# Dealing the last 1024 columns of wq's eighth rows to DMA engines by two indirect loads

## The chip, the cores and the metric

The kernel runs on one core of one Trainium2 chip. The metric is the device time of one execution, in microseconds (us). A core has five engines that run side by side: TensorE (PE), VectorE (DVE), ScalarE (ACT), GpSimd (POOL) and SyncE (SP). SP, ACT and GpSimd also issue DMAs, and these are carried out by 16 DMA engines that the three share.

## The reference, cut to what matters

One decode step for four sequences: an attention block over the last 2048 positions of a cache, then a gated feed-forward block. Layernorm stands in front of both. All inputs are bfloat16.

```python
B, D, Hq, Hkv, Dh, Sk, W, F = 4, 1024, 32, 4, 128, 8192, 2048, 3584
x  = A_x                                   # (4, 1, 1024)
q  = layernorm(x) @ wq                     # wq: (1024, 4096)
s  = q . k_cache[:, :, Sk - W:] * Dh**-0.5 # each of 4 kv heads serves 8 q heads
o  = softmax(s) . v_cache[:, :, Sk - W:]
h  = x + o @ wo                            # wo: (4096, 1024)
n  = layernorm(h)
out = h + (silu(n @ w1) * (n @ w3)) @ w2   # w1, w3: (1024, 3584); w2: (3584, 1024)
```

In all 55.6 MB are read from HBM and 8 KB are written.

## The kernel before

**One stream of weights.** Every weight and cache block goes through one ring in SBUF (`ring`, 128 partitions of 160 KiB). The list `plan` has the loads in order: wq's rows 0 to 3 of each partition, two side loads, wq's rows 4 to 7 (`load_tail`), the four K blocks, the four V blocks, wo, w1, w3 and w2 in four pieces. `load_next` issues the next ones on SP's queue. Seven entries are issued at the start; each later one is issued at a point of the program at which the ring's old contents in its place have been read. In program order SP waits with the load until that reading is done. So w1's issue waits for the attention output of batches 0 and 1 (`OT_ps`, L379), w3's for row 11 of the wo product (L408) and w2's for the wo product and for w1.

**wq.** `wq` is seen as 128 partitions of eight rows: partition p holds rows 8p to 8p + 7, so row 8p + 7 is its eighth row, `kc` = 7. The q product (L263) takes one `kc` after the other. Each time all 128 partitions of the ring meet `xnT[:, kc, :]`, the transposed normalized input, and add into `q_ps` in PSUM: four column groups of 1024 by two halves of 512.

**The side loads.** The last 512 columns of all the eighth rows (`CE` = 512) are left out of `load_tail`. They come by two loads (`load_side`, L120) into tiles of 20 and of 12 partitions, four rows in each partition, 80 + 48 = 128 pieces of 1 KB. To multiply them, the matching elements of `xn` are picked (`xs`, L206), transposed (L211) and copied (`xsT`, L218). Eight matmuls of 20 or 12 rows (L273) add them into `q_ps` after the `kc` = 3 step.

**Behind q.** q is scaled (L281, L282), transposed (L285) and laid out in `qz` (L286). Then K blocks are transposed on TensorE (L319), copied out by VectorE (L322) and multiplied with q (L304). Softmax, the product with V (L379), the wo product (L408), the second layernorm and the feed-forward block (L456, L489) follow. The result goes out by one DMA (L512).

**At the start.** GpSimd makes the identity matrix (`make_identity`, masks.py) and sets `o4` (L237) and `ones` (L242). ACT's queue loads x in two halves (`x_sb`, L158). VectorE clears `x_q`, `q_ps` and `qz`, takes the statistics of x (L180, L182) and normalizes it (L187); TensorE transposes it (L194) and VectorE copies it to `xnT` (L196).

A scheduler decides the order of instructions on each engine from their dependences. Each engine, and each queue, then works through its own list in order.

Of the kernel before, what the change touches and what calls it, by code (L numbers as in the profile page):

```python
# [10 lines left out]
P = 128  # L11
ACT = mybir.ActivationFunctionType
ALU = mybir.AluOpType
AX = mybir.AxisListType
BF16 = mybir.dt.bfloat16
FP32 = mybir.dt.float32


@with_exitstack
def kernel(  # L20
# [13 lines left out]
    nc = tc.nc  # L34

    B, _, D = A_x.shape
# [5 lines left out]
    KC = D // P  # L42
# [15 lines left out]
    ktpool = ctx.enter_context(tc.tile_pool(name="ktpool", bufs=4))  # L58
    wide = ctx.enter_context(tc.tile_pool(name="wide", bufs=2))
    const = ctx.enter_context(tc.tile_pool(name="const", bufs=1))  # L60
    act = ctx.enter_context(tc.tile_pool(name="act", bufs=1))
# [3 lines left out]
    JG = 4  # L65
    QD = P // JG
    RS = QD // B
    CQ = Hq * Dh // JG
# [40 lines left out]
    N_Q, N_F = Hq * Dh, F  # L109


    CE = 512
    SETS = [(0, 5, 4), (80, 3, 4)]

    def load_side(r0, ne, ns):

        t = ktpool.tile([P, JG * QD * 16], BF16, tag="kT")
        rows = A_wq[r0 * KC : (r0 + ne * 4 * ns) * KC, N_Q - CE : N_Q]
        rows = rows.rearrange("(t i k) n -> k i t n", i=ne, k=KC)[KC - 1]
        nc.sync.dma_start(out=t[: ne * 4, : ns * CE], in_=rows)  # L120
        return [t[: ne * 4, k * CE : (k + 1) * CE] for k in range(ns)]

    def load_tail(at, src, n, r0, m):

        t = ring[:, at : at + m * n]
        nc.sync.dma_start(out=t[:, : m * n - CE], in_=src[:, r0 * n : (r0 + m) * n - CE])
        return [t[:, k * n : (k + 1) * n] for k in range(m)]
    KIB = 512
    plan = [
        ("wq", load_rows, (0, wq_v, N_Q, 0, 4)),  # L130
        ("side", load_side, SETS[0]),
        ("side", load_side, SETS[1]),
        ("wq", load_tail, (32 * KIB, wq_v, N_Q, 4, 4)),
        ("k", load_kv, (64 * KIB, A_k_cache, 0)),
        ("k", load_kv, (96 * KIB, A_k_cache, 2)),
# [10 lines left out]
    loaded = {}  # L146
    cursor = [0]

    def load_next(n=1):
        for _ in range(n):  # L150
            if cursor[0] < len(plan):
                kind, f, args = plan[cursor[0]]
                loaded.setdefault(kind, []).extend(f(*args))
                cursor[0] += 1

    x_sb = act.tile([B, D], BF16)
    for c in range(2):
        nc.scalar.dma_start(out=x_sb[:, c * 512 : (c + 1) * 512], in_=x_flat[:, c * 512 : (c + 1) * 512])  # L158
    load_next(7)

    ident = const.tile([P, P], BF16)
    make_identity(nc, ident[:])
    eps_t = const.tile([P, 1], FP32)
    nc.vector.memset(eps_t[:], eps)

# [2 lines left out]
    for c in range(2):  # L168
        nc.sync.dma_start(
            out=x_q[c * 2 * QD : (c + 1) * 2 * QD : RS, :],  # L170
            in_=x_flat.rearrange("b (j c) -> j b c", j=JG)[2 * c : 2 * c + 2],
# [3 lines left out]
    psA = psA_cm.__enter__()  # L175


    stats = act.tile([B, 2, nc.vector.BN_STATS_DIM], FP32)
    for c in range(2):
        nc.vector.bn_stats(out=stats[:, c, :], in_=x_sb[:, c * 512 : (c + 1) * 512])  # L180
    mv = act.tile([B, nc.vector.BN_AGGR_DIM], FP32)
    nc.vector.bn_aggr(out=mv[:], in_=stats[:])  # L182
    rstd = act.tile([B, 1], FP32)
    nc.scalar.activation(out=rstd[:], in_=mv[:, 1:2], func=ACT.Sqrt, bias=eps_t[:B], scale=1.0)
    nc.vector.reciprocal(out=rstd[:], in_=rstd[:])
    xn = act.tile([B, D], BF16)
    nc.vector.tensor_scalar(  # L187
        out=xn[:], in0=x_sb[:], scalar1=mv[:, 0:1], scalar2=rstd[:, 0:1],
        op0=ALU.subtract, op1=ALU.mult,
# [5 lines left out]
    xnT = act.tile([P, KC, B], BF16)  # L195
    nc.vector.tensor_copy(out=xnT[:], in_=tp_ps[:])  # L196


    NS = sum(ns for _, _, ns in SETS)
    ts_ps = psA.tile([P, NS, B], BF16, tag="kt1")  # L200
    xs = wide.tile([B, NS, 20], BF16, tag="w4k")
    sl = []
    for r0, ne, ns in SETS:
        v = xn[:, r0 * KC : (r0 + ne * 4 * ns) * KC]
        v = v.rearrange("b (s l i k) -> b k l i s", s=4, l=ns, i=ne)
        nc.vector.tensor_copy(  # L206
            out=xs[:, len(sl) : len(sl) + ns, : ne * 4].rearrange("b l (i s) -> b l i s", s=4),
            in_=v[:, KC - 1, :, :, :],
        )
        for l in range(ns):  # L210
            nc.tensor.transpose(  # L211
                out=ts_ps[: ne * 4, len(sl), :], in_=xs[:, len(sl), : ne * 4], identity=ident[:B, :B]
            )
            sl.append(ne * 4)
    xsT = act.tile([20, NS, B], BF16)
    k0 = 0
    for _, ne, ns in SETS:
        nc.vector.tensor_copy(out=xsT[: ne * 4, k0 : k0 + ns, :], in_=ts_ps[: ne * 4, k0 : k0 + ns, :])  # L218
        k0 += ns


    q_ps = psA.tile([P, CQ], FP32, tag="scores")
    nc.vector.memset(q_ps[:], 0.0)

    qz = act.tile([P, B, Hkv * QD + REP], BF16)
    nc.vector.memset(qz[:], 0.0)
    ident_f = const.tile([P, P], FP32)
    nc.vector.tensor_copy(out=ident_f[:], in_=ident[:])
# [3 lines left out]
        out=perm[:].rearrange("p (h dq) -> p h dq", dq=JG),  # L232
        in_=ident[:].rearrange("p (dq h) -> p h dq", dq=JG),
    )

    o4 = act.tile([P, IO, B, RS], BF16)
    nc.gpsimd.memset(o4[:], 0.0)  # L237

    mask = const.tile([P, Hkv], FP32)
    nc.vector.reduce_sum(out=mask[:], in_=ident[:].rearrange("p (pp g) -> p g pp", g=Hkv), axis=AX.X)  # L240
# [5 lines left out]
    for j in range(2, JG):  # L246
        nc.vector.tensor_tensor(
            out=same[:, 0, :], in0=same[:, 0, :], in1=ident[:, j * QD : (j + 1) * QD], op=ALU.add
# [6 lines left out]
    for kc in range(KC):  # L255
        wq_t = loaded["wq"][kc]
        for hf in range(CQ // 512):
            for g in range(JG):
                c0 = g * CQ + hf * 512
                n = min(512, N_Q - CE - c0) if kc == KC - 1 else 512  # L260
                if n <= 0:
                    continue
                nc.tensor.matmul(  # L263
                    q_ps[QD * g : QD * g + B, hf * 512 : hf * 512 + n],
                    lhsT=xnT[:, kc, :],
                    rhs=wq_t[:, c0 : c0 + n],
                    start=(kc == 0),
                    stop=(kc == KC - 1 or (kc == KC - 2 and c0 + 512 == N_Q)),
                )
        if kc == RQ - 1:  # L270
            load_next()
            for k, np_ in enumerate(sl):
                nc.tensor.matmul(  # L273
                    q_ps[QD * (JG - 1) : QD * (JG - 1) + B, CQ - CE : CQ],
                    lhsT=xsT[:np_, k, :],
                    rhs=loaded["side"][k],
                    start=False,
                    stop=False,
                )
    q_sb = act.tile([P, CQ], BF16)  # L280
    nc.vector.tensor_single_scalar(out=q_sb[:, :512], in_=q_ps[:, :512], scalar=qscale, op=ALU.mult)  # L281
    nc.scalar.mul(out=q_sb[:, 512:], in_=q_ps[:, 512:], mul=qscale)  # L282
# [1 line left out]
    for r in range(REP):  # L284
        nc.tensor.transpose(out=qt_ps[:, r, :], in_=q_sb[:, r * Dh : (r + 1) * Dh], identity=ident[:])  # L285
    nc.vector.tensor_copy(  # L286
        out=qz[:, :, : Hkv * QD].rearrange("p b (g z) -> p b g z", g=Hkv)[:, :, :, :REP],
        in_=qt_ps[:].rearrange("p r (g x) -> p x g r", g=Hkv)[:, :B, :, :],
# [24 lines left out]
    for u, (b, n) in enumerate(units):  # L313
        k_v = loaded["k"][b]
        kT = ktpool.tile([P, NJ, P], BF16, tag="kT")
        for t in range(NJ // TB):
            kt_ps = psA.tile([P, TB, P], BF16, tag=f"kt{nt % 4}")
            for jj in range(TB):
                nc.tensor.transpose(  # L319
                    out=kt_ps[:, jj, :], in_=k_v[:, n * NJ + t * TB + jj, :], identity=ident[:]  # L320
# [18 lines left out]
        out=Pm[:], in_=scores_ps[:], func=ACT.Exp, bias=nmax[:], scale=1.0, accum_out=rsum[:]  # L339
# [6 lines left out]
    for c in range(NSB):  # L346
# [4 lines left out]
        for g in range(Hkv):  # L351
            if g % 2 == 0:
                nc.vector.tensor_scalar(  # L353
                    out=z[:, :, g, :], in0=pt_ps[:], scalar1=mask[:, g : g + 1], scalar2=None, op0=ALU.mult
# [10 lines left out]
        out=Dm[:], in0=ident[:].rearrange("p (g b r) -> p b g r", g=Hkv, b=B),  # L365
        scalar1=rinv[:, 0:1], scalar2=None, op0=ALU.mult,
# [10 lines left out]
    for b in range(B):  # L377
        for j in range(JK):
            nc.tensor.matmul(  # L379
                OT_ps[:, b, :],  # L380
                lhsT=loaded["v"][b][:, j, :],
                rhs=PTz[j // NJ][:, (j % NJ) * B + b, :, :],
                start=(j == 0),
                stop=(j == JK - 1),
# [21 lines left out]
    for i in range(IO):  # L406
        for j in range(JG):
            nc.tensor.matmul(  # L408
                y_ps[QD * j : QD * (j + 1), :],
                lhsT=o4[:, i, :, :].rearrange("p b s -> p (b s)"),  # L410
                rhs=loaded["wo"][i][:, j * CG : (j + 1) * CG],
                start=(i == 0),
                stop=(i == IO - 1),
# [27 lines left out]
        out=hn[:], in0=h1[:], scalar1=tot[:, 0:1], scalar2=rstd2[:, 0:1],  # L441
        op0=ALU.subtract, op1=ALU.mult,
# [4 lines left out]
        out=hnT[:].rearrange("p k x -> p (k x)"), in_=hn[:].rearrange("q (c k) -> q k c", k=KC)  # L447
# [3 lines left out]
    def gate_up(kind, out_ps):  # L451
# [27 lines left out]
        out=hgT[:].rearrange("p i x -> p (i x)"),  # L479
        in_=hg[:].rearrange("q s c -> q (s c)").rearrange("q (c i) -> q i c", i=IF),  # L480
# [18 lines left out]
    for i in range(R1, IF):  # L499
        for c, t in enumerate((ya_ps, yb_ps)):  # L500
            down(i, HC, c * HC, t, start=(i == R1), stop=(i == IF - 1), skip_group_check=True)
        if i == R2 - 1:
            for c, t in enumerate((ya_ps, yb_ps)):
                nc.tensor.matmul(
                    t[:, :HC], lhsT=ident_f[:], rhs=h2[:, c * HC : (c + 1) * HC],
                    start=False, stop=False, skip_group_check=True,
# [36 lines left out]
```

## Time and profile before

| | us |
|---|---|
| Median of 3 runs | 138.02 (137.87 to 138.12) |
| The profiled execution's own time | 137.67 |
| Its span, first to last instruction | 135.9 |
| First ring load of wq lands, first q matmul | 12.87 |
| Second ring load of wq lands, matmuls go on | 23.61 |
| w1 is issued; its first matmul | 72.82; 98.77 |
| w3's first matmul | 115.67 |
| w2's first matmul | 126.04 |
| Last group of w2 matmuls begins | 132.66 |

Busy shares of the span: TensorE 49%, VectorE 39%, ScalarE 11%, GpSimd 1%; SP's DMA queue holds the 16 DMA engines for 95.6% of it. The page is of one execution, times in us from the span's start. In the row "DMA" each digit is the busy share, in tenths, of one fortieth of the span. The table of DMA queues gives the number of packets, the megabytes, and the time of the packets as a share of 16 engines' span: q1 is SP's queue, q10 is ACT's, q8 and q14 carry instructions. The chain that ended last is followed back from the last instruction, and shown in order of time as start, duration and what. In the timeline each line has start, duration, engine, line of the kernel, operation, output<-inputs, shape and count, and in brackets the idle time before it and what ended that.

### The profile page before, as it was taken

The numbers are of one execution on the slowest core, as the hardware profiler recorded it, in microseconds if no ns is written. First come the engines' busy times: TensorE is split into PE (matmuls) and PEld (weight loads), VectorE is DVE, ScalarE is ACT, GpSimd is POOL, SyncE is SP. The second block draws the span as 40 slices with busy tenths as digits, with TensorE's granted clock in tenths as the row PEclk, the third lists the DMA queues.
The fourth block names the chain that finished last, engine by engine and source line by source line (L and its number), as shares of the span: only waits on it lengthen the run. The fifth ranks groups of instructions, "written<-read, shape, count | busy, mean of one in ns | idle before, by whom it ended". The sixth has DMA issues, their size and how long they took to land.

```text
span 135.9 us, 2420 instructions
## 1 busy us (share of the span) xinstructions
PE 66.7 (49%) x1096; PEld 42.1 (31%) x1096; DVE 53.2 (39%) x95; ACT 15.1 (11%) x20; POOL 1.7 (1%) x8
## 2 busy tenths in 40 slices
PE   0004930979898989105259155930094000940961
PEld 0002210266656565001149053720041000410750
DVE  6056000069696969709940003044000893052010
ACT  3000000010000000092943000000005000000000
POOL 5000000000000000000000000000000000000000
PEclk9999985699999999955555955599559955599599
DMA  5999999999999999999989999989989899899970
GB/s 156 464 463 415 404 430 405 434 424 439 420 439 415 434 439 415 424 550 439 482 347 444 487 405 410 439 376 490 456 371 477 354 490 408 379 451 399 414 317 2
DMA packets 2649, 55.74 MB, mean 410 GB/s; under 512 B 296, under 2 KB 464, under 8 KB 720
## 3 DMA queue, kind: packets, MB, share of 16 engines
q1 hardware_dynamic: 2604, 55.58, 95.6%
q8 instruction: 8, 0.13, 0.3%
q10 hardware_dynamic: 36, 0.02, 0.1%
q14 instruction: 1, 0.01, 0.0%
HBM read 55.59 MB, written 0.01 MB: 409 GB/s over the span
## 4 chain that ended last, share of the span: by engine, by line
DMA 57%; PE 22%; DVE 10%; ACT 6%; SPq 2%; issue 1%; ACTq 0%
DMA ring<-in_B_w_dram 42%; DMA ring<-in_A_wq_dram 15%; PE kt_ps L319 10%; PE scores_ps L304 5%; DVE kT L322 4%; DVE z L353 3%; ACT z L357 3%; PE q_ps L263 2%; PE g_ps L456 2%; DVE rmax L333 2%; ACT Pm L338 2%; PE OT_ps L379 1%; DVE pT L347 1%; SPq L120 1%; ACT L338 1%
## 5 line engine op out<-in xcount | busy, mean ns | idle before, releaser
L322 DVE COPY kT<-kt_ps 128x1024 bf16<-128x1024 bf16 x32 | 20.2, 685 | 5.2 <-PE kt_ps L319 5.0
L319 PE MATMUL kt_ps<-ident,ring 128*128 128x128 bf16 x256 | 16.5, 219 | 0.0
L319 PEld LDWEIGHTS <-ring 128*128 128x128 bf16 x256 | 14.4, 98 | 5.0 <-issue 4.9
L379 PE MATMUL OT_ps<-z,ring 128*128 128x32 bf16 x256 | 7.5, 186 | 9.6 <-ACT z L357 5.0
L456 PEld LDWEIGHTS <-hnT 128*32 128x32 bf16 x128 | 4.6, 121 | 24.0 <-issue 20.6
L304 PE MATMUL scores_ps<-kT,qz 128*32 128x512 bf16 x64 | 9.9, 609 | 1.7 <-DVE kT L322 1.5
L456 PE MATMUL u_ps<-ring,hnT 128*32 128x448 bf16 x64 | 4.6, 459 | 12.4 <-DMA ring<-in_B_w_dram 12.4
L379 PEld LDWEIGHTS <-ring 128*128 128x128 bf16 x256 | 7.3, 103 | 10.3 <-issue 10.2
L263 PE MATMUL q_ps<-ring,xnT 128*4 128x512 bf16 x63 | 6.8, 603 | 7.3 <-DMA ring<-in_A_wq_dram 7.3
L456 PE MATMUL g_ps<-ring,hnT 128*32 128x448 bf16 x64 | 4.5, 455 | 7.4 <-DMA ring<-in_B_w_dram 7.4
L489 PEld LDWEIGHTS <-hgT 128*32 128x32 bf16 x156 | 4.1, 113 | 8.2 <-issue 7.6
L281 DVE TENSOR_SCALAR q_sb<-q_ps 128x512 bf16<-128x512 f32 x1 | 0.7, 692 | 14.3 <-PE q_ps L263 14.3
L489 PE MATMUL y_ps<-ring,hgT 128*32 128x256 bf16 x68 | 3.4, 382 | 5.8 <-DMA ring<-in_B_w_dram 5.8
L408 PE MATMUL y_ps<-ring,o 128*32 128x256 bf16 x128 | 5.7, 364 | 0.8 <-DVE o L395 0.8
L353 DVE TENSOR_SCALAR z<-pt_ps,mask 128x512 bf16<-128x512 f32 x8 | 5.5, 740 | 1.1 <-ACT z L357 0.8
L470 DVE RECIPROCAL eg<-eg 128x896 f32<-128x896 f32 x1 | 5.8, 5752 | 0.0
L357 ACT ACTIVATE z<-pt_ps,mask 128x512 bf16<-128x512 f32 x8 | 5.4, 687 | 3.4 <-DVE z L353 3.4
L349 PE MATMUL pt_ps<-pT,perm 128*128 128x512 bf16 x4 | 2.4, 608 | 6.8 <-DVE pT L347 6.8
L194 PE MATMUL tp_ps<-ident,xn 4*128 4x4 bf16 x8 | 0.7, 199 | 10.0 <-DVE xn L187 10.0
L263 PEld LDWEIGHTS <-xnT 128*4 128x4 bf16 x63 | 2.1, 116 | 11.2 <-issue 11.1
L469 DVE TENSOR_SCALAR eg<-eg 128x896 f32<-128x896 f32 x1 | 0.6, 627 | 12.1 <-ACT eg L468 12.1
L408 PEld LDWEIGHTS <-o 128*32 128x32 bf16 x128 | 4.3, 129 | 3.0 <-DVE o L395 1.9
(84 smaller groups left out, 47.1 us busy)
## 6 DMA issues: line engine op xcount, KB each, us to landing
ring<-in_B_w_dram SPq DMA_DIRECT2D x2, 7168.0 KB, 25.9
ring<-in_A_k_cache_dram SPq DMA_DIRECT2D x4, 2048.0 KB, 27.6
ring<-in_A_v_cache_dram SPq DMA_DIRECT2D x4, 2048.0 KB, 29.1
ring<-in_B_w_dram SPq DMA_DIRECT2D x1, 4352.0 KB
ring<-in_A_wq_dram SPq DMA_DIRECT2D x1, 4096.0 KB, 12.1
ring<-in_A_wq_dram SPq DMA_DIRECT2D x1, 3968.0 KB
ring<-in_B_w_dram SPq DMA_DIRECT2D x1, 1792.0 KB
ring<-in_B_w_dram SPq DMA_DIRECT2D x1, 768.0 KB
```

Source lines behind the costliest of these rows:

```text
L263: nc.tensor.matmul(q_ps[QD * g : QD * g + B, hf * 512 : hf * 512 + n], lhsT=xnT[:, kc, :], rhs=wq_t[:, c0 : c0 + n], start=(kc == 0), stop ...
L304: nc.tensor.matmul(scores_ps[QD * g : QD * (g + 1), n * 512 : (n + 1) * 512], lhsT=qz_v[:, z0 : z0 + QD], rhs=kT_v[:, g, :, :], start=(b = ...
L319: nc.tensor.transpose(out=kt_ps[:, jj, :], in_=k_v[:, n * NJ + t * TB + jj, :], identity=ident[:])
L322: nc.vector.tensor_copy(out=kT[:, t * TB : (t + 1) * TB, :], in_=kt_ps[:])
L338: nc.scalar.activation(out=Pm[:], in_=scores_ps[:], func=ACT.Exp, bias=nmax[:], scale=1.0, accum_out=rsum[:])
L353: nc.vector.tensor_scalar(out=z[:, :, g, :], in0=pt_ps[:], scalar1=mask[:, g : g + 1], scalar2=None, op0=ALU.mult)
L357: nc.scalar.mul(out=z[:, :, g, :], in_=pt_ps[:], mul=mask[:, g : g + 1])
L379: nc.tensor.matmul(OT_ps[:, b, :], lhsT=loaded["v"][b][:, j, :], rhs=PTz[j // NJ][:, (j % NJ) * B + b, :, :], start=(j == 0), stop=(j == J ...
L408: nc.tensor.matmul(y_ps[QD * j : QD * (j + 1), :], lhsT=o4[:, i, :, :].rearrange("p b s -> p (b s)"), rhs=loaded["wo"][i][:, j * CG : (j + ...
L456: nc.tensor.matmul(out_ps[QD * j : QD * (j + 1), hf, :HF], lhsT=hnT[:, k, :], rhs=loaded[kind][k][:, c0 : c0 + HF], start=(k == 0), stop=( ...
L470: nc.vector.reciprocal(out=eg[:], in_=eg[:])
L489: nc.tensor.matmul(out_ps[QD * j : QD * (j + 1), :n], lhsT=hgT[:, i, :], rhs=loaded["w2"][i][:, j * CG + c0 : j * CG + c0 + n], **kw,)
```

## The change

The eighth rows lose their last 1024 columns (`CX`) in the ring load. These come as 128 pieces of 2 KB by two indirect loads on GpSimd's queue, into a tile `xg` of 128 partitions and two layers. `DEAL` lists, for each of the two loads, which runs of slots (partitions of `xg`) take a piece: 82 slots in the first load and 46 in the second. The wq rows are numbered off into these slots in order.

The matrix `sel` has a one where row m goes to slot s, and is copied together from columns of the identity on GpSimd. A matmul of `sel` with the row numbers minus 256 (`pv`) gives each slot its row number, from which VectorE computes the block index (`idf`, `idx`). A slot without a row gets an index past `bounds_check`, and is left out by the load. A matmul of `sel` with `xnT[:, 7, :]` gives each slot its factor of x (`xgT`), zero for empty slots, and `xg` is cleared at the start. Four matmuls over 128 slots add the product into `q_ps`, behind the `kc` = 7 step.

With it go: the side loads, their picking, transposes, copies and matmuls. One more of the last row's matmuls goes (both halves of the last column group are now left out). The clearing of `o4` moves from GpSimd to VectorE, and the normalization's `stats` tile shares its buffer with `idf`.

In the changed program's lists, VectorE has the clearing of `xg` first, and `idf` and `idx` ahead of the statistics of x. GpSimd has `sel`'s clearing, the identity, the row numbers, `ones`, twelve copies into `sel`, the cast of the row numbers and then the two loads. SP's list is the same without the two side loads. TensorE begins with the two matmuls for the indices.

```diff
-    CE = 512
-    SETS = [(0, 5, 4), (80, 3, 4)]
-    def load_side(r0, ne, ns):
-        t = ktpool.tile([P, JG * QD * 16], BF16, tag="kT")
-        rows = A_wq[r0 * KC : (r0 + ne * 4 * ns) * KC, N_Q - CE : N_Q]
-        rows = rows.rearrange("(t i k) n -> k i t n", i=ne, k=KC)[KC - 1]
-        nc.sync.dma_start(out=t[: ne * 4, : ns * CE], in_=rows)
-        return [t[: ne * 4, k * CE : (k + 1) * CE] for k in range(ns)]
+    CX = 1024
+    DEAL = [
+        [(0, 40), (48, 6), (56, 8), (64, 7), (72, 5), (80, 8), (120, 8)],
+        [(0, 24), (32, 8), (56, 1), (80, 5), (120, 8)],
+    ]
 def load_tail(at, src, n, r0, m):
-        nc.sync.dma_start(out=t[:, : m * n - CE], in_=src[:, r0 * n : (r0 + m) * n - CE])
+        nc.sync.dma_start(out=t[:, : m * n - CX], in_=src[:, r0 * n : (r0 + m) * n - CX])
 plan = [
-        ("side", load_side, SETS[0]),
-        ("side", load_side, SETS[1]),
...
+    sel = wide.tile([P, 2, P], BF16, tag="w4k")
+    nc.gpsimd.memset(sel[:], 0.0)
+    m0 = 0
+    for e, deal in enumerate(DEAL):
+        for at, n in deal:
+            nc.gpsimd.tensor_copy(out=sel[:, e, at : at + n], in_=ident[:, m0 : m0 + n])
+            m0 += n
+    pidx = const.tile([P, 1], I32)
+    nc.gpsimd.iota(pidx[:], pattern=[[0, 1]], base=-2 * P, channel_multiplier=1)
+    pv = const.tile([P, 1], BF16)
+    nc.gpsimd.tensor_copy(out=pv[:], in_=pidx[:])
+    xg = ktpool.tile([P, 2, CX], BF16, tag="kT")
+    nc.vector.memset(xg[:], 0.0)
...
+    NB = KC * N_Q // CX
+    id_ps = psA.tile([P, 2], FP32, tag="kt3")
+    for e in range(2):
+        nc.tensor.matmul(id_ps[:, e : e + 1], lhsT=sel[:, e, :], rhs=pv[:], start=True, stop=True)
+    idf = act.tile([P, 2], FP32, tag="stats")
+    nc.vector.tensor_scalar(
+        out=idf[:], in0=id_ps[:], scalar1=float(NB), scalar2=float(2 * P * NB + NB - 1),
+        op0=ALU.mult, op1=ALU.add,
+    )
+    idx = const.tile([P, 2], I32)
+    nc.vector.tensor_copy(out=idx[:], in_=idf[:])
+    for e in range(2):
+        nc.gpsimd.indirect_dma_start(
+            out=xg[:, e, :], out_offset=None, in_=A_wq.rearrange("r (t c) -> (r t) c", c=CX),
+            in_offset=bass.IndirectOffsetOnAxis(ap=idx[:, e : e + 1], axis=0),
+            bounds_check=P * NB - 1, oob_is_err=False,
+        )
...
+    xg_ps = psA.tile([P, 2, B], FP32, tag="kt2")
+    for e in range(2):
+        nc.tensor.matmul(xg_ps[:, e, :], lhsT=sel[:, e, :], rhs=xnT[:, KC - 1, :], start=True, stop=True)
+    xgT = act.tile([P, 2, B], BF16)
+    nc.vector.tensor_copy(out=xgT[:], in_=xg_ps[:])
...
-    nc.gpsimd.memset(o4[:], 0.0)
+    nc.vector.memset(o4[:], 0.0)
...
-            for k, np_ in enumerate(sl):
-                nc.tensor.matmul(
-                    q_ps[QD * (JG - 1) : QD * (JG - 1) + B, CQ - CE : CQ],
-                    lhsT=xsT[:np_, k, :],
-                    rhs=loaded["side"][k],
-                    start=False,
-                    stop=False,
-                )
+    for e in range(2):
+        for hf in range(CQ // 512):
+            nc.tensor.matmul(
+                q_ps[QD * (JG - 1) : QD * (JG - 1) + B, hf * 512 : (hf + 1) * 512],
+                lhsT=xgT[:, e, :],
+                rhs=xg[:, e, hf * 512 : (hf + 1) * 512],
+                start=False,
+                stop=(e == 1),
+            )
```

## The prediction

> **What bounds the kernel now.** I read the page's DMA rows and queue table first, then the chain that ended last in order of time, then the timelines of the queues and of GpSimd.
>
> ```profile
> DMA  5999999999999999999989999989989899899970
> q1 hardware_dynamic: 2604, 55.58, 95.6%
> q8 instruction: 8, 0.13, 0.3%
> ...
> 3.03 20.54 DMA ring<-in_A_wq_dram
> 23.61 3.28 PE q_ps L263 x30
> ...
> 72.82 25.91 DMA ring<-in_B_w_dram
> 98.77 2.41 PE g_ps L456 x16
> 101.19 0.07 SPq L94
> 101.26 0.05 issue
> 101.31 31.31 DMA ring<-in_B_w_dram
> 132.66 0.24 PE ya_ps L489 x4
> ```
>
> The DMA engines are busy in every slice; from 72.82 on, the chain is two waits for weights, and only 0.3 us of TensorE work follows the last landing. So the time is when the slowest of the 16 DMA engines has moved its share, plus a fixed end: 135.9 - 132.32 us of the span behind the last landing and 1.77 us outside the span (137.67 for this execution). The median of the runs shown is 138.02, 0.35 above it; I work against 137.67 and carry the difference to 138.02.
>
> The page gives no view by DMA engine, so I took the trace's packet records (start, duration, size, queue) and chained each packet to the one whose end meets its start. Sixteen chains come out, each with the same eight rows of every ring load. Rows run at one pace: 32,768 bytes in 1.213 us, 31,744 in 1.175, 2,048 in the last load every 0.080, the side loads' 1,024 every 0.042. The chains end at: eleven between 131.96 and 132.32, one at 131.28, four between 130.59 and 130.90; mean 131.77. They differ by four things:
> - start of the first packet and a few slower ones: 12.05 to 12.50 us at the end of the first load;
> - side pieces: three chains carry 32 of 1,024 bytes (1.35 us), two carry 16 (0.67 us);
> - a 16,384-byte fetch of the instruction queue (q8), before 125 us on seven other chains: a gap of 0.9 to 1.0 us and a next packet 0.5 us longer, 1.4 us in all; the eighth, at 130.90, begins when one of the early chains has just ended;
> - one 8,192-byte instruction fetch at 51.5 us, 0.31 + 0.53 us, on a chain with 16 side pieces.
>
> So the early chains have neither side pieces nor a fetch. A perfect deal of the same bytes would end all at 131.77, 0.55 us sooner. That is the whole prize, 0.4%.
>
> **The change, part by part.** *Shorter tail rows.* Each engine's eight rows shrink from 31,744 to 30,720 bytes: 8 x 1.175 x 1,024/31,744 = 0.30 us off every chain.
>
> *The side loads go.* 1.35 us off three chains, 0.67 off two.
>
> *128 pieces of 2,048 bytes come.* At 0.080 us each. The sizes in DEAL stand on multiples of 8 slots; I read 8 consecutive slots as one engine's. Then engines 0, 1, 2, 4 and 15 get 16 pieces, 10 gets 13, 7 gets 9, 3 gets 8, 8 gets 7, 6 gets 6, 9 gets 5, and 5 and 11 to 14 none. The total is unchanged (128 x 0.080 = 10.2 us, against 128 x 0.042 + 16 x 0.30 = 10.2). The chains with side pieces must be five named engines, and I take them as 0 to 4. The three heavy ones: 132.32, 132.20, 132.31, less 1.35 and 0.30, plus 16 x 0.080 = 1.28: 131.95, 131.83, 131.94. The one with the half fetch (132.23): less 0.67 and 0.30, plus 8 x 0.080: 131.90; the other, with 16: 131.59. Four of five stand within 0.12 us of each other: the pieces fill just the delays that the trace shows. For the other eleven the trace has no engine's name. If they fit as well, the latest are full-fetch chains with no piece: 132.25 - 0.30 = 131.95. Two more completion writes per engine (9 ns packets, gaps of as much) add 0.03. End 131.98 against 132.32: -0.34 us, 137.33 for the profiled execution, 137.68 for the median.
>
> The Trainium skill, "DMA: Bandwidth & Descriptors", section "The descriptor swizzle", speaks against my reading: it gives engine 8*(p>>6) + ((p>>2)&7), four slots of one half and four from 32 further on. By that rule the engines that I count at 0 pieces would get up to 10 (engine 5), so 131.95 + 0.80, a slower kernel by 0.43 us. No row of before can tell, since an SP load of 128 rows gives each engine eight either way.
>
> *What a piece costs on GpSimd's queue* isn't in this trace. Below: 0.076, the bytes at the ring's rate. Above: 0.084, a packet's own duration in the last load, plus perhaps a fetch of its descriptor, for which the 4-byte packets' 0.009 is the nearest row: 0.093. Sixteen pieces then end 0.06 earlier or 0.21 later; I take 0.080, the same size in the same trace. A skipped slot costs 0 as I read it, at most a piece's 0.080 (see the rivals).
>
> *GpSimd's list in front of the indirect loads.*
>
> ```profile
> 0.73 0.85 ACTq L158 DMA_DIRECT2D x_sb<-in_A_x_dram  x2
> 0.87 0.95 POOL L237 MEMSET o<- 128x1024 bf16 x1
> 1.17 1.81 SPq L120 DMA_DIRECT2D t<-in_A_wq_dram  x2
> 1.85 0.29 POOL masks.py:199 TENSOR_SCALAR_AFFINE_SELECT ident<-ident 128x128 bf16<-128x128 bf16 x1
> 8.00 0.68 DVE L180 BATCH_NORM_STATS2 stats<-x_sb 4x6 f32<-4x512 bf16 x1 [4.87 <-DMA x_sb<-in_A_x_dram]
> 16.30 1.89 PE L273 MATMUL q_ps<-t,xsT 20*4 20x512 bf16 x8
> 40.36 0.34 SPq L94 DMA_DIRECT2D ring<-in_A_wo_dram  x1
> ```
>
> The memset of o4 moves to VectorE; sel's, a quarter of it, takes about 0.3. Twelve copies, an iota and a cast: each between 0.10 (the smallest memset) and 0.29 (affine select), so 1.4 to 4.1 us, done at 4 to 6.7. Two matmuls and two small VectorE steps add 0.7: indices at 4.7 to 7.4. New wait: VectorE stands at idf, and bn_stats is queued behind it. The second bn_stats waits for its half of x until 8.00 anyway, so this costs nothing; uncovered it would still have 1.9 us until the first wq rows at 12.87. SP is two issues (1.81 us) shorter; the ring's first 4 MB keeps the engines busy until 12.05, so nothing moves.
>
> *When the pieces land.* The second half of x was issued by 1.6 and started at 6.06, behind four ring packets: the nearest row. Two issues of 0.8 to 1.0 (SP's for the side loads) and four packets (4.9 us) put the first pieces at about 11.5 to 14. The nearest bounds for the rest: all 16 back to back (1.3 us), or one ring packet before each: some seven behind tail rows of 1.14 and nine behind k rows of 0.61, so at about 28.5. TensorE would take them at 26.3, so between 0 and 2.2 us late; I take the middle, on time or 1 us late. What covers it: this chain's next gate is the issue of w1 at 72.82 behind OT_ps, while wo keeps even the earliest engine busy until 79.72. Issue to first packet is 1.0 us at the start (0.73 to 1.74), so 5.9 us of slack. The issue of wo (40.36) has over 15.
>
> The Trainium skill, the same page, section "Queues, rings and completion order", says that an engine takes turns between its queues by whole packets of many descriptors. Were an engine's eight pieces one packet, they would land near 16 us; the four ring packets ahead of x agree with turns, the trace doesn't show a packet's size on this queue.
>
> *TensorE and VectorE.* Eight transposes, eight side matmuls (1.89 us at 16.30, followed by 5.4 us of idleness) and one last-row matmul go; two plus two small matmuls come, and four of 0.11 us right before q_sb, +0.33 on that chain, within the 5.9. The kernel has nine matmuls fewer, so instruction fetches come up to nine matmuls later in the program; whether they land on the same engines is the open point.
>
> **The rivals.**
> - *The fetches don't match the deal.* The trace has seven full fetches among the eleven unnamed chains, the deal has only five empty engines there. If that stays, two full-fetch chains carry at least 5 and 6 pieces: at best 131.76 + 0.40 and 131.66 + 0.48, about 132.16, or -0.16 us; with 9 on one, 132.6, +0.3. 137.85 to 138.3, likeliest 137.95. For: the count. Against: the pieces with 5 to 9 fit engines with a half fetch, as on the one I can name.
> - *The pieces go elsewhere (slower).* The slots fall on the engines in another way, or skipped slots move bytes too. Spread evenly, 128 pieces are eight for each full-fetch chain: 131.95 + 0.64, +0.27; with skipped slots moving bytes all have 16: 131.95 + 1.28, +0.91. So 138.3 to 138.95. It decides from seven pieces on a full-fetch chain (131.95 + 0.56, +0.2).
> - *The pieces land late.* After 26.3 + 5.9 = 32.2 us the engines run dry before w1, and each us more is a us: from two ring packets before each piece on. Over 139.
>
> **The numbers.** Forecast 0.46, fetches that don't match 0.22, pieces elsewhere 0.22, late 0.10. A difference of 0.2% (0.28 us) is about what a measurement of this kernel can tell. The forecast's -0.34 is just past it, with 0.1 either way from the piece's cost and rounding: 0.4 faster, 0.06 same; the second case gives 0.05 faster, 0.13 same, 0.04 slower; the others are slower. Faster 0.45, same 0.19, slower 0.36. The range goes from 137.4, under the perfect deal's 137.47 by a spread of the runs, to 138.9, near the end of pieces elsewhere; 137.5 to 137.85 is the forecast's own.
>
> **What would show it.** Right: sixteen chains that end within 0.4 us, the latest near 131.98; tail rows of 1.14 us; pieces of about 0.080 on eleven chains and none on five; q_sb before 32; w1's issue before 78. Wrong: pieces on chains with a full fetch; a piece every 0.1 us or more; pieces on all sixteen; a gap in the DMA row before w1; bn_stats behind idf after 8.7.

## The result and the profile after

The changed kernel takes 138.50 us (median of 8 runs, 138.39 to 138.99) against 137.88 (median of 8 runs, 137.84 to 138.12) on the same chip: +0.62 us. The ratio is 1.0049, 95% interval 1.0035 to 1.0063. The forecast was 137.68, faster; it went the way of the second rival, "the pieces go elsewhere" (138.3 to 138.95).

The page of the changed kernel, its DMA row and its queues:

```profile
span 136.7 us, 2420 instructions
...
DMA  5998998999999999999999999999999898998950
...
q1 hardware_dynamic: 2468, 55.32, 94.6%
q0 software_dynamic: 160, 0.26, 0.5%
q8 instruction: 8, 0.13, 0.3%
```

The DMA row is about as full as before, so nothing ran dry. q0 is GpSimd's queue, new in this kernel: 160 packets, 0.26 MB. The eight instruction fetches (q8) are still there.

The start, from the timeline of the changed kernel:

```profile
1.70 1.63 POOL L163 COPY sel<-ident 128x40 bf16<-128x40 bf16 x12
...
4.62 0.17 DVE L196 CAST idx<-idf 128x2 int32<-128x2 f32 x1
...
5.07 1.19 POOL L198 DMA_INDIRECT xg<-in_A_wq_dram,idx  x1 [1.61 <-DVE same L258]
6.57 1.00 POOL L198 DMA_INDIRECT xg<-in_A_wq_dram,idx  x1 [0.30 <-issue]
7.94 0.68 DVE L207 BATCH_NORM_STATS2 stats<-x_sb 4x6 f32<-4x512 bf16 x1 [2.44 <-DMA x_sb<-in_A_x_dram]
...
26.83 0.69 DVE L292 TENSOR_SCALAR q_sb<-q_ps 128x512 bf16<-128x512 f32 x1 [15.53 <-PE q_ps L284]
```

The twelve copies take 1.63 us. The indices are ready at 4.8, the statistics wait for x as before (7.94 against 8.00), and q is scaled at 26.83 against 26.91. The last packet of the pieces ends at 21.25, well ahead of the matmul that reads it at 25.61. None of the loss is here.

The end, from the chain that ended last in the changed kernel (start, duration, what):

```profile
72.87 26.55 DMA ring<-in_B_w_dram
99.41 0.04 issue
99.45 1.68 PE g_ps L467 x12
101.14 29.68 DMA ring<-in_B_w_dram
...
132.86 0.17 PE ya_ps L500 x4
...
133.31 0.22 PE ya_ps L500 x4
```

w1 is issued at 72.87 (72.82 before): the q path moved nothing. w1's first matmul is 0.68 us later (99.45 against 98.77), the last group 0.65 us later (133.31 against 132.66). The last part of this chain runs through TensorE, whose granted clock was 0.50 from 126 to 131 us here. That is a tie: the weights' last packet ends at 132.94 (before 132.33), its completion comes at 133.25, and TensorE is done with the group before it just then, at 133.31. The clock is not the cause of the loss, for three runs of the changed kernel with a mean granted clock of 0.80 took 138.46, 138.48 and 138.61 us, as long as the others. The slowest DMA engine is 0.61 us later. Chained as in the prediction, the 16 ends now have their mean near 131.9 (131.77 before), and the four latest stand between 132.82 and 132.94. All four have a full instruction fetch (16,384 bytes) and, as far as chains that cross can be told apart, five or more pieces. The deal made the latest engines later.

A second thing shows at the very end: from the landing of the output to the end of the span it is 1.02 us, against 0.84 before. Behind that landing SP's closing list has three waits of 0.06 us each where it had one, and GpSimd's clearing of semaphores takes 0.14 us instead of 0.10. (The kernel without the loads, below, also has three, and 0.96 us.) So 0.61 from the weights and 0.18 from the ending make the 0.8 us between the two spans. The profiled execution of before was one of its fastest; between medians it is 0.62.

### The profile page after: what moved, and what is told of

Read it like the earlier page. It is cut to its first block, busy times and chain, and to the rows that moved or that the text cites. A ratio compares the mean times of both kernels' runs of the same rounds, so it can differ in the third digit from the quotient of the medians.

```text
span 136.7 us, 2420 instructions
## 1 busy us (share of the span) xinstructions
PE 68.9 (50%) x1087; PEld 44.0 (32%) x1087; DVE 53.7 (39%) x96; ACT 15.1 (11%) x20; POOL 5.1 (4%) x24
## 4 chain that ended last, share of the span: by engine, by line
DMA 57%; PE 24%; DVE 9%; ACT 7%; issue 1%; SPq 0%; DVEq 0%; ACTq 0%
DMA ring<-in_B_w_dram 41%; DMA ring<-in_A_wq_dram 16%; PE kt_ps L330 10%; PE scores_ps L315 5%; DVE kT L333 4%; ACT z L368 3%; PE q_ps L273 2%; DVE rmax L344 2%; DVE z L364 2%; ACT Pm L349 2%; PE OT_ps L390 1%; DVE pT L358 1%; PE g_ps L467 1%; PE ya_ps L500 1%; ACT L349 1%
## 5 line engine op out<-in xcount | busy, mean ns | idle before, releaser
L467 PEld LDWEIGHTS <-hnT 128*32 128x32 bf16 x128 | 5.4, 140 | 25.8 <-issue 23.2
L467 PE MATMUL u_ps<-ring,hnT 128*32 128x448 bf16 x64 | 5.7, 546 | 11.3 <-DMA ring<-in_B_w_dram 11.3
L467 PE MATMUL g_ps<-ring,hnT 128*32 128x448 bf16 x64 | 5.6, 540 | 8.9 <-DMA ring<-in_B_w_dram 8.9
L500 PEld LDWEIGHTS <-hgT 128*32 128x32 bf16 x156 | 4.7, 128 | 6.5 <-issue 5.7
L419 PEld LDWEIGHTS <-o 128*32 128x32 bf16 x128 | 5.0, 132 | 3.9 <-issue 3.2
```

Source lines behind the costliest of these rows:

```text
L419: nc.tensor.matmul(y_ps[QD * j : QD * (j + 1), :], lhsT=o4[:, i, :, :].rearrange("p b s -> p (b s)"), rhs=loaded["wo"][i][:, j * CG : (j + ...
L467: nc.tensor.matmul(out_ps[QD * j : QD * (j + 1), hf, :HF], lhsT=hnT[:, k, :], rhs=loaded[kind][k][:, c0 : c0 + HF], start=(k == 0), stop=( ...
L500: nc.tensor.matmul(out_ps[QD * j : QD * (j + 1), :n], lhsT=hgT[:, i, :], rhs=loaded["w2"][i][:, j * CG + c0 : j * CG + c0 + n], **kw,)
```

## The experiments

Every experiment ran beside the kernel before on one chip, but not all on the same chip, so experiments are compared by their ratios to it where the chips differ. Theory A: the pieces go to engines by another slot rule than I read, and fall on engines that carry an instruction fetch. Rival B: GpSimd's queue costs all engines time, wherever the pieces go. Rival C: an instruction fetch may come on any engine in any execution, so that no deal can fit.

**The changed kernel again** (no edit).

> The changed kernel once more, for a second profile. Theory A (pieces of the indirect loads go to an engine by groups of four slots, four of one group and four from 32 further on, and so fall on engines that also carry an instruction fetch): 138.5, about +0.6 us to before; the instruction fetches come on the same engines as in the first profile (eleven 16-slot patterns of full and empty slots tell most engines apart), and the four latest chains end near 132.9. Rival C (the engine of a fetch is a matter of the execution): the fetches come on other engines, the latest chains are others, and the time moves by some tenths. Rival B (the GpSimd queue costs every engine time): says the same 138.5 here.

138.49 (5 runs), ratio 1.0039, interval 1.0026 to 1.0052. The last packet ends at 132.87. The third and the seventh fetch fall on chains with the same patterns of slots in both profiles (those that the rule gives to engines 13 and 9). Most other chains have patterns in common or cross too closely to be told apart, so C was left to the next kernels.

**The meant numbers of pieces, slots by the other rule.** Engine e < 8 is given slots 4e to 4e + 3 and 32 + 4e to 32 + 4e + 3, the others the same from 64 on:

```diff
     DEAL = [
-        [(0, 40), (48, 6), (56, 8), (64, 7), (72, 5), (80, 8), (120, 8)],
-        [(0, 24), (32, 8), (56, 1), (80, 5), (120, 8)],
+        [(0, 20), (24, 28), (56, 2), (60, 16), (92, 7), (100, 1), (104, 4), (124, 4)],
+        [(0, 12), (16, 4), (28, 1), (32, 12), (48, 4), (72, 4), (92, 4), (104, 1), (124, 4)],
     ]
```

> The same numbers of pieces for each engine that the change meant under my first reading (16, 16, 16, 8, 16, 0, 6, 9, 7, 5, 13, 0, 0, 0, 0, 16 for engines 0 to 15), but with the slots chosen by the other rule (four slots, and four from 32 further on). If the rule is right, the profile shows four packets of 4 KB per load on engines with 16 pieces. Theory A with fetches as in the first profile of the changed kernel (full fetches on 4, 6, 7, 9, 11, 13 and 14 or 15): engine 4 then has a fetch and 16 pieces, 131.8 + 16 x 0.088 = 133.2, so about 138.8, +0.9 to before. If the fetches come elsewhere and match these numbers, 131.95, about 137.5. Rival B: the deal matters little, 138.4 to 138.6.

138.77 (5 runs), ratio 1.0058, interval 1.0045 to 1.0072. Two pieces share a packet of 4,096 bytes, two skipped slots a packet of 8. Written per chain (F two pieces, h one piece and a skipped slot, a dot two skipped slots, a bar the completion), with fetches and the end of the last packet:

```
engine      slots of load 1|load 2  fetch at us        end us
0,1,2,4,15  FFFF|FFFF|              -                  131.57 to 132.22
3           FFFF|....|              51.3 (8 KB)        132.10
5,11 to 14  ....|....|              one each: 32.7,    131.58 to 132.16
                                    42.9, 54.4, 77.4,
                                    83.7
6           FFF.|....|              90.7               132.43
7           FFFFh...|               -                  131.00
8           FFFh|....|              -                  131.05
9           FFh.|....|              105.2              132.16
10          FFFF|FFh.|              131.1              133.00
```

Every engine has just the pieces that the rule gives it, which eight consecutive slots to an engine would not: the slot rule is shown. And the numbers in DEAL now make sense: the five engines meant to stay empty all carry a full fetch. Engines 7 and 8 could have held more, 6 a little less. But the time is set at one place, engine 10. Its 13 pieces were to fill it up, but the eighth fetch found it at work: after two of its last eight 2 KB packets comes the fetch, 0.93 us, and the next three take 0.23 each instead of 0.08. The kernel's last group of matmuls waits for that engine's last packet:

```profile
133.47 0.24 PE ya_ps L500 x4
```

The time itself, 138.77, is the 138.8 expected, but by luck: that was to come from a fetch and 16 pieces on engine 4, and no fetch fell on engine 4. Why the eighth fetch cut in here is open. In the kernel before and in the even, the clean and the opposite deal below it starts, to within 0.01 us, where one chain ends: at 130.90, 131.40, 130.48 and 131.33. In the even kernel the code names that chain as engine 10's.

**Eight pieces for every engine,** with another pattern of slots for each engine, so that they can be named:

```diff
-    for e, deal in enumerate(DEAL):
-        for at, n in deal:
-            nc.gpsimd.tensor_copy(out=sel[:, e, at : at + n], in_=ident[:, m0 : m0 + n])
+    # bit j of the engine's number: its slot pair j is full in load 0, else in load 1
```

> Eight pieces for every engine, and in each load another pattern of full and empty pairs of slots for each of the 16 engines, so that every engine's chain can be named in the trace. Theory A: no engine is relieved, the full-fetch chains end at their ends of before or later: 131.9 to 132.4 without pieces + 8 x 0.088 = 132.6 to 133.1, 138.2 to 138.7. Rival B: as the changed kernel, 138.5. Theory A also says that the chains without a fetch end 1.4 us before the others.

138.62 (5 runs), ratio 1.0047, interval 1.0033 to 1.006. Chains with a fetch end at 132.28 to 132.81, those without at 130.90 to 131.48; the mean is 131.91. The codes that can be read for sure name the engine of the second fetch, 12, and of the fourth to seventh: 14, 5, 6 and 9; the 8 KB fetch is on 3. All are in the set of the re-dealt kernel. Rival C falls for these programs: their fetches keep to the same engines. The changed kernel (138.50) is no better than this deal, which relieves nobody.

**No pieces.**

```diff
-    for e in range(2):
-        nc.gpsimd.indirect_dma_start(...)
```

> The two indirect loads are left out (the last 1024 columns of the eighth rows are missing from the product); all else of the changed kernel stays. 0.26 MB less is read. Theory A: the latest chain is a full-fetch chain without pieces, 131.95 to 132.4: 137.5 to 137.95, 0.55 to 1.0 below the changed kernel. Rival B (the queue itself, with its descriptors and completions, costs each engine): over 1.0 below, 137.4 or less, and all chains, also those that had one to four pieces, end sooner by more than 0.3 us.

137.57 (6 runs), ratio 0.9969, interval 0.9957 to 0.9981: 0.92 below the changed kernel on the same chip. The mean end of the chains is 131.18 (131.91 in the even kernel): eight pieces, with the queue's skipped slots and completions, cost 0.73 us, 0.091 a piece. The latest chains all have full fetches, the last ends at 132.25. Add 0.091 for every piece that the rule gives such an engine in the changed kernel: by the order of the fetches 12 has 8 pieces (132.25 + 0.73 = 132.98), 14 has 8 (132.64), 5 has 10 (132.60) and 6 has 9 (132.56). The largest sum meets the 132.94 measured. The others are too small: by their patterns the chains of 5 and 6 ended at 132.89 and 132.86 in the changed kernel. These are single executions of two programs, and the chains do not start alike in them, so the one match is no more than a check of the size.

**Pieces on clean engines alone** (16 each on 0, 1, 2, 4, 7, 8, 15; 8 on 3; 4 each on 5 and 6):

```diff
+        [(0, 52), (60, 8), (92, 8), (124, 4)],
+        [(0, 12), (16, 4), (28, 16), (48, 4), (60, 8), (92, 8), (124, 4)],
```

> The slots are chosen by the four-and-four rule, and the pieces go to the seven engines that no instruction fetch hit in the profiles of the re-dealt and even kernels (0, 1, 2, 4, 7, 8 and 15, 16 pieces each), 8 to engine 3 (the 8 KB fetch), 4 each to 5 and 6 and none to 9 to 14. Theory A: the latest chains are then full-fetch chains without pieces, 131.95 to 132.25, as with no pieces at all: 137.6 to 137.75, 0.2 to 0.35 below before and 0.75 to 0.9 below the changed kernel. Rival B (the queue costs every engine, the deal little): 138.3 to 138.6. Rival C (the engine of a fetch changes from program to program): 138.5 or more, since a clean engine hit by a fetch would end at 133.3.

138.13 (11 runs), ratio 1.0022, interval 1.0013 to 1.003. By the ratios this is 0.2 to 0.4 us better than the changed kernel (1.0049 and 1.0039), but short of the 137.6 to 137.75 expected. In the trace the deal does what it should: the last packet ends at 132.37, the last group starts at 132.70, 0.04 later than before.

```profile
101.37 31.29 DMA ring<-in_B_w_dram
132.66 0.04 issue
132.70 0.24 PE ya_ps L500 x4
```

So the weights land as in the kernel before, and the time is still 0.3 longer. Of this 0.18 is the ending, 1.02 us again from the output's landing. About 0.1 is not in one profiled execution's weights or ending, and stays open.

**Engine 10 relieved in the re-dealt kernel** (13 pieces from 10, of which 9 to 8 and 4 to 7):

```diff
-        [(0, 20), (24, 28), (56, 2), (60, 16), (92, 7), (100, 1), (104, 4), (124, 4)],
-        [(0, 12), (16, 4), (28, 1), (32, 12), (48, 4), (72, 4), (92, 4), (104, 1), (124, 4)],
+        [(0, 20), (24, 28), (56, 2), (60, 12), (92, 9), (124, 4)],
+        [(0, 12), (16, 4), (28, 16), (48, 4), (60, 1), (64, 4), (92, 8), (124, 4)],
```

> The re-dealt kernel (138.77) with one thing moved: engine 10's 13 pieces go to 7 and 8 (13 and 16 there, none on 10). In the re-dealt kernel engine 10 was last, at 133.0, because the eighth instruction fetch found it still at work on its last eight packets. Theory A: the latest is then engine 6, fetch and 6 pieces, near 132.4: 137.8 to 138.0, 0.8 to 0.95 below the re-dealt kernel. Rival B: 138.5 to 138.8, no change.

138.19 (9 runs), ratio 1.0023, interval 1.0013 to 1.0032. The re-dealt kernel was 0.82 us above the kernel before on its chip, this one is 0.36 above it: 0.46 gained, where 0.8 was expected. The last packet ends at 132.35 instead of 133.00. The eighth fetch now comes to an engine that has ended its share at 130.57.

**The opposite deal** (16 each on the seven engines with a full fetch, 8 on 3 and 10):

```diff
+        [(12, 4), (20, 8), (44, 4), (52, 8), (68, 24), (100, 24)],
+        [(20, 8), (52, 8), (68, 4), (76, 16), (100, 4), (108, 16)],
```

> The opposite deal: 16 pieces each on the seven engines with a full fetch (5, 6, 9, 11, 12, 13, 14), 8 on 3 and on 10. Theory A: 131.7 to 132.25 + 16 x 0.091 = 133.2 to 133.7: 139.0 to 139.3, and seven chains end near 130.4. Rival B: 138.4 to 138.6. By the first reading (eight consecutive slots to an engine) the load is spread: engines get 4 to 16 pieces in another order.

139.19 (4 runs), ratio 1.0095, interval 1.008 to 1.0109. The last packets end at 133.65 and seven chains at 130.2 to 130.7, as theory A has it. Between this deal and the clean one lie 1.06 us on the same chip, with the same loads and bytes and twelve copies into `sel` instead of eleven: the deal matters, rival B does not explain the loss.

```profile
102.58 31.34 DMA ring<-in_B_w_dram
133.92 0.04 issue
133.97 0.24 PE ya_ps L500 x4
```

**Eight pieces each by one plain load on ACT's queue:**

```diff
+    nc.scalar.dma_start(out=xg[:, 0, :],
+        in_=A_wq.rearrange("(p k) n -> k p n", k=KC)[KC - 1][:, N_Q - CX :])
-        nc.gpsimd.indirect_dma_start(...)
```

> Eight pieces for each engine as in the even kernel, but by one plain load on ACT's queue instead of two indirect ones on GpSimd's; the selection matmuls stay. It measures what the queue and its packets cost. Theory A with a cost of 0.091 us for a piece on GpSimd's queue against 0.080 on a hardware queue: 0.1 us below the even kernel (138.62), 138.5. Rival B: the queue costs more than its bytes, 0.4 us or more below, 138.2 or less.

138.51 (6 runs), ratio 1.0054, interval 1.0041 to 1.0067. The same as the even kernel (1.0047, 1.0033 to 1.006) within the spread: no cost of GpSimd's queue over ACT's can be seen.

**Empty loads** (all 256 slots skipped):

```diff
-        out=idf[:], in0=id_ps[:], scalar1=float(NB), ...
+        out=idf[:], in0=id_ps[:], scalar1=0.0, ...
```

> The changed kernel with every index past the bound: both indirect loads are issued, all 256 slots are skipped, no piece moves (the last 1024 columns of the eighth rows are missing from the product, as in the kernel with no pieces, 137.57). What is left is the queue's own cost: skipped slots, completions, and two more waits at the end of the program. Theory A, with a fixed cost seen at the end of the clean-engine kernel (0.18 us from the last landing to the end, 0.96 to 1.02 against 0.84 in before): 137.7 to 137.9. Rival B (the queue costs every engine much more): 138.1 or more.

137.78 (11 runs), ratio 0.9992, interval 0.9983 to 1.0001; the kernel without the loads had 0.9969. The queue itself costs 0.2 to 0.3 us. The page of this kernel shows what a skipped slot is:

```profile
q0 software_dynamic: 160, 0.00, 0.1%
```

Of the 160 packets 128 hold 8 bytes, for two skipped slots each, and 32 hold the 4 bytes of a completion; each takes about 9 ns. The last weights end as without the loads (132.19 against 132.25) and the ending is 0.06 longer (1.02 against 0.96); the rest of the 0.2 can't be seen in one profiled execution.

**One full load instead of two half-full ones,** `DEAL = [[(0, 128)]]` and one pass in each loop.

> One indirect load with all 128 slots full, eight pieces for every engine, instead of the even kernel's two half-full ones (138.62). Theory A (a piece costs its bytes, a load only its completions and a wait at the end): 138.4 to 138.6, at most 0.2 below. Rival B (the load itself is dear): 138.2 or less.

138.56 (5 runs), ratio 1.0058, interval 1.0044 to 1.0071, against 1.0047 for two. The number of loads costs nothing that shows.

No version here beats the kernel before with the whole product computed. The best, the clean deal, is at 1.0022.

## Why the prediction was wrong

**The step that failed** is "I read 8 consecutive slots as one engine's". The engine goes by four slots and four more from 32 further on. The Trainium skill, "DMA: Bandwidth & Descriptors", section "The descriptor swizzle", gives this rule for a transfer to 128 partitions, and the prediction cited it as speaking against its reading; the packets of the re-dealt and even kernels agree with it chain by chain. By it the changed kernel gives 16, 16, 8, 8, 12, 10, 9, 8, 4, 3, 4, 1, 8, 5, 8 and 8 pieces to engines 0 to 15. Engines 5, 11, 12, 13 and 14, which I counted at none, get 10, 1, 8, 5 and 8. The rival's price, 131.95 + 8 x 0.080 = 132.59 or more, was 0.35 short of the 132.94 measured, since the latest chain without pieces ended at 132.25 and a piece cost 0.091. Mending this step alone would not have brought the gain: the re-dealt kernel, with the meant numbers on the meant engines, is at 1.0058.

**"If they fit as well" was half right.** The prediction had four of five named chains that fit, and took the other eleven to fit too. With the slots put right, the numbers do fit the fetches of engines 3, 5, 9 and 11 to 14, and engine 6 within 0.3 us. What I left out is the eighth fetch. I had seen it, at 130.90, "when one of the early chains has just ended", and priced it at nothing. With 13 pieces on it, engine 10 ended at 133.00 in the re-dealt kernel, and 0.46 us came back when they went elsewhere.

**"132.25 - 0.30 = 131.95" was too early for the latest full-fetch chain.** Without any piece, 0.26 MB less to read, the latest ended at 132.25. It had ended its first load at 12.67, later than any chain of before (12.50). The shorter tail rows were there, but the chains did not start as in before, and the sum held their starts fixed. Even the kernel that leaves out the pieces was only 0.31% faster than before; with them, 0.25% was forecast.

**The first rival** (seven full fetches, five empty engines) counted rightly: engines 6 and 9 carry a fetch and pieces even in the meant deal, and 6 ended at 132.43.

**The ending behind the last landing was taken as fixed.** It grew by 0.18 us, two more closing waits and a longer clearing of semaphores. That alone is half of the gain forecast. 0.12 of it stays in the kernel without the loads, so it belongs to the change as a whole more than to its queue.

**Right:** the tail rows (1.138 us measured, 1.137 by proportion); GpSimd's list (indices at 4.8 of 4.7 to 7.4); no cost from the new wait of VectorE; pieces on time (completions by 21.25, where 26.3 was needed); the q path's slack, with w1 issued 0.05 us later; a skipped slot at next to nothing. A piece's own packet time was right too, 0.159 for two, 0.0795 each; all told a piece delayed the mean end by 0.091. The engines took turns by packets of two pieces, so the eight of a chain did not land together.

## What to carry to other kernels

When 16 DMA engines share a stream and the slowest sets the time, chain the trace's packets by engine before moving bytes between engines, and prove with a coded pattern (as in the even kernel) which slot goes to which engine. An engine that ends early is not always free: here an instruction fetch ran on it right after its last packet, and with 13 pieces there the fetch fell among the last packets. And a gain of a few tenths must also pay for what a change adds to the program's closing waits.

## What the runs showed of the hardware

- Instruction fetches are a load on single DMA engines: 16 KB take 0.88 to 1.03 us, and the next packet of the stream takes about 0.5 us longer (2.61 to 2.67 us instead of 2.12 for 57,344 bytes), 1.4 us in all. In the re-dealt kernel they came on engines 5, 6, 9 and 11 to 14, the last on 10, and 8 KB on 3, and the other kernels dealt by the rule agree where their patterns can be read. What picks these engines wasn't tried.
- On GpSimd's queue each engine moved one packet, two pieces of 2 KB in 0.159 us, between two ring packets most of the time: in the re-dealt kernel a chain with 16 pieces went 30,720 bytes in 1.138 us, 4,096 in 0.159, and so on. Eight such packets spread over some 10 us.
- A skipped slot of an indirect load still has 4 bytes in the trace; two of them share a 9 ns packet (128 packets of 8 bytes for 256 slots, all skipped).
